# Two attention layers on one core: constants and casts in parts, DMA transposes for the later row tiles, and a new order table

## The chip, the cores and the metric

The kernel runs on one core of one Trainium2 chip. The metric is device time in microseconds of one execution; the time before is the median of three runs. One execution was also recorded by the hardware profiler, and every line of a profile shown here is from such a record.

## The reference

Inputs are q, k and v of shape 4 x 8 x 768 x 64 (batch, heads, rows, head size) in float32, and the weights of a second layer. The first layer is attention with a window: a row sees the 8 first keys (the global ones) and the 96 keys up to its own. A slope per head times the distance is taken off the scores.

```python
keep = is_global | is_local
dist = np.where(is_global & ~is_local, float(n_local), np.abs(rel))
scores = np.where(keep, scale * q @ k.T - slopes * dist, -1e9)
x = softmax(scores) @ v            # then heads side by side: 4 x 768 x 512
```

The second layer is a mixture of four attention experts of head size 64 with causal attention over all rows. A gate picks two experts per row, and their outputs are weighted with the softmax of the two gate values.

```python
q, k, v = x @ wq[e], x @ wk[e], x @ wv[e]
ye = softmax(causal(q @ k.T / 8)) @ v @ wo[e]
out += w[row, e] * ye              # for the two experts of the row
```

## The kernel before

The 4 x 768 rows are 24 row tiles of 128 rows, numbered u = 0 to 23, six per batch. Each tile runs through the same stages, and each stage is a small function with a two-letter name.

First layer: load k, q and v of the tile (lk, lq, lv), 256 KB each; cast them to float16 (kc, qc, vc); transpose k and q on TensorE into PSUM and copy both into kqT (tk, tq; `turn`, L266 and L275); local scores in two halves with the bias added by a matmul (sa, sb; L335, L342, exponential at L345); global scores for up to three tiles at a time (gs); values (vg, va, vb; L356, L371), with the division by the row sum at L378 and L380, which gives x16. Transposed x is made by `turn_x` (tx; L386 on TensorE, copy at L390).

Second layer: keys and queries of the four experts (pk, pq; L401, copy at L406), values and gate logits (pv; L415, L417, L421), the routing in small steps (ro), causal scores in up to three parts (ca, cb, cc; L446, exponential at L449), the mask (ma; L461 on GpSimd), values (za, zb; L474) and the weighting L481, L483 and L485, which gives zs. Transposed zs is made by `turn_z` (tz; L491, copy at L495). The output projection (ou; L502, copy at L505) ends with a store issued from SyncE (L506).

The order of all work is written out in a table of slots, `ORDER`; the tile framework keeps this order on every engine and adds the waits. A slot is a stage, a number and, where the stage has a choice, a letter for the engine: a is ScalarE, g is GpSimd, v is VectorE; for loads s is SyncE's DMA queue and a is ScalarE's. So `tx5v` transposes x of tile 5 and has the copy done by VectorE. What stands earlier in the table stands earlier in the queue of every engine that it uses; a wait holds back what follows on that engine alone.

The weights are loaded by wi and cast by wc. In the kernel before, row kp*4+ko of a weight goes to partition kp, so a partition reads 1 KB in a row, and `turn_x` picks every fourth column of x to match:

```python
issue(w32s[i][:, :, :, :].rearrange("p e k d -> p e (k d)"),
      (moe_wk, moe_wq, moe_wv)[i].rearrange("e (kp ko) d -> kp e (ko d)", ko=NK))
```

Constants are made at the start: the bias of the local scores (xb), and in one function the mask and bias of the global keys, the mask of the keys and the selection matrix (xg), all on VectorE. Buffers `abuf` are zeroed on VectorE (az). `keep_warm` (wm) runs matmuls whose result is not used. PSUM tiles for transposes, projections and outputs share two buffers (psT). After the table a check of all row sums (L753 to L763) decides whether a general path, which is not taken here, has to run.

## Time and profile before

| what | value |
|---|---|
| median of 3 runs | 153.75 us (152.28 to 154.81) |
| the profiled execution | 154.6 us |
| its span | 151.9 us |
| TensorE matmuls | 2987, 137.3 us busy |
| VectorE, ScalarE, GpSimd busy | 111.3, 105.6, 94.6 us |
| DMA | 27.81 MB in 80376 packets |
| transposes on TensorE | 192 of k and q, 96 of x, 48 of z |
| granted TensorE clock | 0.986 |

The span is what the profile covers; the profiled execution is 2.7 us longer than it. TensorE matmuls are pipelined, so the busy time of a run of them is longer than the time that it adds; the spacing of their starts is the better measure. Lines such as L401 are lines of the kernel before. PEld is the loading of a stationary operand, PEq or SPq the sequencer of an engine.

### The profile page before, as it was taken

How to read it: one execution, taken by the hardware profiler on the slowest of the kernel's cores; microseconds unless marked ns; L12 is line 12 of the kernel's file. 1: busy time of each engine (PE TensorE's matmuls, PEld its weight loads, DVE VectorE, ACT ScalarE, POOL GpSimd, SP SyncE). 2: the span in 40 equal slices, each digit the busy share in tenths (PEclk: the TensorE clock that was granted, in tenths of full speed). 3: DMA queues.
4: the chain of work that ended last, by engine and by line, in shares of the span. 5: the costliest groups of instructions: out<-in, count | busy, mean ns of one | idle time of the engine just before them, and what ended most of it. 6: DMA issues, size and time to landing. Idle time of an engine off the chain costs nothing.

```text
span 151.9 us, 7115 instructions
## 1 busy us (share of the span) xinstructions
PE 137.3 (90%) x2987; PEld 107.5 (71%) x2987; DVE 111.3 (73%) x343; ACT 105.6 (70%) x174; POOL 94.6 (62%) x258
## 2 busy tenths in 40 slices
PE   5889969989999998899999999999999999999700
PEld 4556747768789786787787887788868987856300
DVE  6976958577887984888759788797867787797610
ACT  0345656666879887498786877869796988898410
POOL 4492896484888785749889789543786444544000
PEclk9999999999999999999999999999999999999995
DMA  4999999979899898999994994345013003116540
GB/s 106 284 288 291 353 231 279 265 177 277 195 276 233 199 239 184 204 285 223 316 242 103 261 222 135 84 147 134 4 69 145 4 4 140 73 48 230 194 167 11
DMA packets 80376, 27.81 MB, mean 183 GB/s; under 512 B 75472, under 2 KB 77008, under 8 KB 80336
## 3 DMA queue, kind: packets, MB, share of 16 engines
q1 hardware_dynamic: 65632, 23.60, 60.0%
q10 hardware_dynamic: 14704, 3.68, 10.8%
q8 instruction: 25, 0.41, 1.1%
q14 instruction: 15, 0.12, 0.3%
HBM read 20.98 MB, written 6.29 MB: 180 GB/s over the span
## 4 chain that ended last, share of the span: by engine, by line
PE 61%; DMA 11%; DVE 9%; POOL 9%; issue 3%; ACT 2%; POOLq 0%; ACTq 0%; DVEq 0%
DMA qf<-in_q_dram 11%; PE pps L401 10%; PE zps L474 7%; PE ops L502 7%; PE vps L415 6%; PE cps L446 6%; PE zps L371 4%; PE sps L335 4%; POOL vbuf L258 4%; PE tp L266 4%; PE xps L386 3%; PE sps L342 3%; PE ztps L491 2%; PE zps L356 2%; POOL s16q L250 1%
## 5 line engine op out<-in xcount | busy, mean ns | idle before, releaser
L449 ACT ACTIVATE a<-cps 128x1024 f16<-128x1024 f32 (+1 forms) x48 | 42.0, 916 | 4.0 <-PE cps L446 3.6
L258 POOL CAST vbuf<-vf 64x256 f16<-64x256 f32 x92 | 37.0, 402 | 6.6 <-DMA vf<-in_v_dram 2.6
L345 ACT ACTIVATE abuf<-sps 128x636 f16<-128x636 f32 (+1 forms) x48 | 30.7, 683 | 9.1 <-PE sps L342 8.7
L461 POOL TENSOR_SCALAR_AFFINE_SELECT a<-a 128x256 f16<-128x256 f16 x48 | 18.4, 411 | 12.8 <-ACT a L449 12.8
L275 DVE COPY kqT<-tp 128x1024 f16<-128x1024 f16 x23 | 15.5, 686 | 5.3 <-PE tp L266 5.1
L380 DVE TENSOR_TENSOR x<-zps,rinv 128x512 f16<-128x512 f32 x24 | 16.6, 691 | 0.8
L474 PE MATMUL zps<-v2buf,a 128*128 128x65 f16 x336 | 15.4, 193 | 0.2
L371 PE MATMUL zps<-vbuf,abuf 64*128 64x65 f16 x704 | 15.2, 189 | 0.0
L335 PE MATMUL sps<-biasT,ident 64*64 64x318 f16 (+1 forms) x192 | 14.8, 313 | 0.1
L401 PE MATMUL pps<-xT,wk 128*128 128x128 f16 x192 | 14.6, 219 | 0.1
L401 PE MATMUL pps<-xT,wq 128*128 128x128 f16 x192 | 14.5, 219 | 0.0
L474 PEld LDWEIGHTS <-a 128*128 128x128 f16 x336 | 12.9, 97 | 2.1 <-DVE zs L485 0.8
L371 PEld LDWEIGHTS <-abuf 64*128 64x128 f16 x704 | 13.9, 94 | 0.6
L342 PE MATMUL sps<-kqT 64*64 64x159 f16 (+2 forms) x384 | 14.2, 228 | 0.0
L415 PE MATMUL vps<-wvg,xT 128*128 128x260 f16 x96 | 13.6, 275 | 0.0
L502 PE MATMUL ops<-wo,zt 128*128 128x512 f16 x48 | 13.2, 380 | 0.4 <-DVE zt L495 0.4
L250 POOL CAST s16k<-kf 128x512 f16<-128x512 f32 x17 | 10.3, 609 | 5.2 <-DMA kf<-in_k_dram 3.3
L446 PE MATMUL cps<-kq,kq 64*128 64x128 f16 x240 | 13.2, 217 | 0.0
L446 PEld LDWEIGHTS <-kq 64*128 64x128 f16 x336 | 9.9, 94 | 4.5 <-issue 3.4
L401 PEld LDWEIGHTS <-wk 128*128 128x128 f16 x192 | 11.5, 98 | 1.8 <-issue 0.2
L342 PEld LDWEIGHTS <-kqT 64*64 64x64 f16 x384 | 11.4, 108 | 1.1 <-issue 0.2
L401 PEld LDWEIGHTS <-wq 128*128 128x128 f16 x192 | 11.6, 98 | 0.1
(112 smaller groups left out, 272.9 us busy)
## 6 DMA issues: line engine op xcount, KB each, us to landing
out_dram<-osb SPq DMA_DIRECT2D x24, 256.0 KB, 2.1
qf<-in_q_dram SPq DMA_DIRECT2D x20, 256.0 KB, 5.0
vf<-in_v_dram SPq DMA_DIRECT2D x20, 256.0 KB, 5.2
kf<-in_k_dram SPq DMA_DIRECT2D x18, 256.0 KB, 5.1
kf<-in_k_dram ACTq DMA_DIRECT2D x6, 256.0 KB, 5.3
vf<-in_v_dram ACTq DMA_DIRECT2D x4, 256.0 KB, 5.8
qf<-in_q_dram ACTq DMA_DIRECT2D x4, 256.0 KB, 6.0
w<-in_moe_wk_dram SPq DMA_DIRECT2D x1, 512.0 KB, 5.1
```

Source lines behind the costliest of these rows:

```text
L258: copies[on](o[hf * KB:(hf + 1) * KB, c, :, 0:Dh], fs["v", u][c * KB:(c + 1) * KB, hf * HG:(hf + 1) * HG, :])
L335: mm(s_ps[o, hh, 0:2 * w].rearrange("r (c n) -> r c n", c=2), lhsT=ident2[r, :], rhs=biasT[r, p, 0:w].unsqueeze(1).to_broadcast([KB, 2, w] ...
L342: mm(s_ps[o, hh, c * w:c * w + n], lhsT=kqT[b][r, 0, p, k0:k0 + KB], rhs=kqT[b][r, 1, p, k0:k0 + n], start=False, stop=True, skip_group_ch ...
L345: S_.activation(as_[u][:, :, g, :].rearrange("r h (c n) -> r h c n", c=2)[:, :, :, 0:w], s_ps[:, :, 0:2 * w].rearrange("r h (c n) -> r h c ...
L371: mm(zs_[u][:, hf, hq * VW:(hq + 1) * VW], lhsT=as_[u - prev][r, hq % 2, hq // 2, at:at + P], rhs=held("vbuf", u - prev)[r, c, hq, :], sta ...
L401: mm(p_ps[:, i, ep, :], lhsT=w[:, ko, ep, :, :].rearrange("r a d -> r (a d)"), rhs=xT[:, ko, :], start=(i == 0 and ep == 0 and ko == 0), s ...
L415: mm(v_ps[:, :], lhsT=xT[:, ko, :], rhs=wvg16[:, ko, :], start=(ko == 0), stop=(ko == NK - 1))
L446: mm(s_ps[:, e2, i, :], lhsT=kqs[b * NT + ci][r, 0, ep, :], rhs=kqs[u][r, 1, ep, :], start=(i == 0), stop=True, skip_group_check=True)
L449: S_.activation(a2[:, :, 4 * c:4 * c + len(part), :], s_ps[:, :, 0:len(part), :], func=Exp, scale=sc2)
L461: G.affine_select(out=d, in_=d, pattern=[[0, NEP], [1, P]], channel_multiplier=-1, base=0, compare_op=Alu.is_ge, fill=0.0)
L474: mm(z_ps[:, e, :], lhsT=a2[:, e % 2, (e // 2) * n + ci, :], rhs=held("v2buf", b * NT + ci)[:, e, :], start=(e == 0 and ci == 0), stop=Tru ...
L502: mm(o_ps[:, :], lhsT=zts[u][:, ep, :], rhs=wo16[:, ep, :], start=(ep == 0), stop=(ep == NEP - 1))
```

## The change

Constants: the two constant functions are cut into smaller stages (xb, xi, xm, xc, xk, xs), most with a letter for the engine, and the index for the upper 64 rows is made by a second iota instead of an addition. `local_zeros` takes a letter. The value cast is cut into two stages of two halves each (vc and vx).

Transposes: `turn`, `turn_x` and `turn_z` take the letter s, which issues one DMA transpose from SyncE's queue, from SBUF to SBUF, with no PSUM tile and no copy. The table uses it for x and z of tiles 12 to 22, and for q and k of tiles 16 to 23. Since it takes columns as they stand, the weights are now loaded with row ko*128+kp on partition kp, in pieces of 256 bytes, and TensorE's transposes of x take plain columns as well. x16 gets 5 buffers and xT 4 (3 each before). The general path uses the weights of the fast path instead of its own copies.

Table: `ORDER` is written anew. Of the loads, 28 are issued from ScalarE's queue instead of 14. `xt` (the early request for the exponential's table) stands last.

```diff
@@ -72,62 +72,71 @@
     sel = const.tile([P, H // 2, KB], F16)
     warm = const.tile([P, 1], F32)
     V.memset(warm[:, :], 0.0)
+    engines = {"g": G, "v": V}
     rel_i = const.tile([P, W], I32)
-    G.iota(rel_i[:, :], pattern=[[1, W]], channel_multiplier=-1, base=0)
+    for r in (slice(0, KB), slice(KB, P)):
+        G.iota(rel_i[r, :], pattern=[[1, W]], channel_multiplier=-1, base=0)
     row_i = const.tile([P, 1], I32)
     G.iota(row_i[:, :], pattern=[[0, 1]], channel_multiplier=1, base=0)
     col_i = const.tile([P, P], I32)
     G.iota(col_i[:, :], pattern=[[1, P]], channel_multiplier=0, base=0)
 
     def bias_constants(_):
-        up = slice(KB, P)
-        V.tensor_copy(rel[0:KB, :], rel_i[0:KB, :])
-        V.tensor_scalar(rel[up, :], rel_i[up, :], float(KB), None, op0=Alu.add)
+        V.tensor_copy(rel[:, :], rel_i[:, :])
         ge = const.tile([P, W], F32, name="ge")
         V.tensor_scalar(ge[:, :], rel[:, :], 0.0, None, op0=Alu.is_ge)
         lt = const.tile([P, W], F32, name="lt")
         V.scalar_tensor_tensor(lt[:, :], rel[:, :], float(NL), ge[:, :],
                                op0=Alu.is_lt, op1=Alu.mult)
         V.tensor_scalar(lt[:, :], lt[:, :], -1.0, -NEG, op0=Alu.add, op1=Alu.mult)
-        V.tensor_scalar(rel[up, :], rel[up, :], slopes[1] / slopes[0], None, op0=Alu.mult)
+        V.tensor_scalar(rel[KB:P, :], rel[KB:P, :], slopes[1] / slopes[0], None, op0=Alu.mult)
         for p in range(NP):
             V.scalar_tensor_tensor(biasT[:, p, :], rel[:, :], -slopes[2 * p] / sc1, lt[:, :],
                                    op0=Alu.mult, op1=Alu.add)
-        for r in (slice(0, KB), up):
-            V.tensor_copy(ident2[r, :], ident[r, r])
-
-    def global_constants(_):
-
+
+    def half_identities(_, on):
+        for r in (slice(0, KB), slice(KB, P)):
+            copies[on](ident2[r, :], ident[r, r])
+
+
+    def global_mask(_, on):
+        e = engines[on]
         key_i = const.tile([P, 1], I32, name="key_i")
         V.tensor_scalar(key_i[:, :], row_i[:, :], NG - 1, None, op0=Alu.bitwise_and)
         key_f = const.tile([P, 1], F32, name="key_f")
         V.tensor_copy(key_f[:, :], key_i[:, :])
-        col_f = const.tile([P, P], F32, name="col_f")
-        V.tensor_copy(col_f[:, :], col_i[:, :])
         grel = const.tile([P, P], F32, name="grel")
-        V.tensor_scalar(grel[:, :], col_f[:, :], key_f[:, :], None, op0=Alu.subtract)
+        e.tensor_copy(grel[:, :], col_i[:, :])
+        e.tensor_scalar(grel[:, :], grel[:, :], key_f[:, :], None, op0=Alu.subtract)
         g_lo = const.tile([P, P], F32, name="g_lo")
-        V.tensor_scalar(g_lo[:, :], grel[:, :], 0.0, NEG, op0=Alu.is_ge, op1=Alu.mult)
-        V.scalar_tensor_tensor(gmask[:, :], grel[:, :], float(NL), g_lo[:, :],
-                               op0=Alu.is_lt, op1=Alu.mult)
+        e.tensor_scalar(g_lo[:, :], grel[:, :], 0.0, NEG, op0=Alu.is_ge, op1=Alu.mult)
+        e.tensor_scalar(grel[:, :], grel[:, :], float(NL), None, op0=Alu.is_lt)
+        e.tensor_tensor(gmask[:, :], grel[:, :], g_lo[:, :], op=Alu.mult)
+
...
+    def selection(_, on):
+
+        G.memset(sel[:, :, :], 0.0)
         for hq in range(HG):
             at = hq // 2 * 32 + hq % 2 * NG
-            V.tensor_copy(sel[:, hq, at:at + NG], ident2[:, 0:NG])
+            copies[on](sel[:, hq, at:at + NG], ident2[:, 0:NG])
 
 
     rinv1 = const.tile([P, B, NT, H], F32)
@@ -146,13 +155,12 @@
         issue = queues[on]
         if i == 4:
             w32s[i] = wst.tile([P, NK, E], F32, name="wg32", tag="wg32", bufs=1)
-            issue(w32s[i][:, :, :].rearrange("p k e -> p (k e)"),
-                  moe_w_gate.rearrange("(kp ko) e -> kp (ko e)", ko=NK))
+            issue(w32s[i][:, :, :], moe_w_gate.rearrange("(ko kp) e -> kp ko e", kp=P))
             return
         w32s[i] = wst.tile([P, E, NK, Hd], F32, name="w32", tag="w32")
         if i < 3:
-            issue(w32s[i][:, :, :, :].rearrange("p e k d -> p e (k d)"),
-                  (moe_wk, moe_wq, moe_wv)[i].rearrange("e (kp ko) d -> kp e (ko d)", ko=NK))
+            issue(w32s[i][:, :, :, :],
+                  (moe_wk, moe_wq, moe_wv)[i].rearrange("e (ko kp) d -> kp e ko d", kp=P))
         else:
             issue(w32s[i][:, :, :, :].rearrange("p e k d -> p (e k d)")
                   .rearrange("p (a m) -> p a m", a=NEP),
@@ -213,9 +221,9 @@
 
     abufs = [big.tile([P, 2, 2, WA], F16, name=f"abuf{i}") for i in range(NA)]
 
-    def local_zeros(i):
-        V.memset(abufs[i][:, :, :, W:2 * P], 0.0)
-        V.memset(abufs[i][:, :, :, 2 * P + W:WA - KB], 0.0)
+    def local_zeros(i, on):
+        engines[on].memset(abufs[i][:, :, :, W:2 * P], 0.0)
+        engines[on].memset(abufs[i][:, :, :, 2 * P + W:WA - KB], 0.0)
 
     ring("vbuf", NV, [2, HG, VW], Dh)
     ring("v2buf", NV2, [E, VW], Hd)
@@ -249,30 +257,32 @@
         s16s[nm, u] = pp.tile([P, H, Dh], F16, name="s16" + nm)
         copies[on](s16s[nm, u][:, :, :], fs[nm, u][:, :, :])
 
-    def cast_v(u, on):
-
-
-        o = take("vbuf", u)
+    def cast_v(u, x, on):
+
+
+
+        o = held("vbuf", u) if x else take("vbuf", u)
         for hf in range(2):
-            for c in range(2):
+            for c in (hf ^ x,):
                 copies[on](o[hf * KB:(hf + 1) * KB, c, :, 0:Dh],
                            fs["v", u][c * KB:(c + 1) * KB, hf * HG:(hf + 1) * HG, :])
 
     def turn(u, i, on=None):
 
+
+        b, ri = divmod(u, NT)
+        if b not in kqT:
+            kqT[b] = pp.tile([P, 2, NP, S], F16, name="kqT", bufs=2)
+        s16 = s16s["kq"[i], u][:, :, :].rearrange("j h d -> j (h d)")
+        if on == "s":
+            nc.sync.dma_start_transpose(kqT[b][:, i, :, ri * P:(ri + 1) * P], s16)
+            return
         if i == 0:
             tps[u] = psT.tile([P, 2, NP, P], F16, name="tp", tag="t")
         for p in range(NP):
-            nc.tensor.transpose(
-                tps[u][:, i, p, :],
-                s16s["kq"[i], u][:, 2 * p:2 * p + 2, :].rearrange("j h d -> j (h d)"),
-                ident[:, :])
-        if i == 0:
-            return
-        b, ri = divmod(u, NT)
-        if ri == 0:
-            kqT[b] = pp.tile([P, 2, NP, S], F16, name="kqT", bufs=2)
-        copies[on](kqT[b][:, :, :, ri * P:(ri + 1) * P], tps[u][:, :, :, :])
+            nc.tensor.transpose(tps[u][:, i, p, :], s16[:, p * P:(p + 1) * P], ident[:, :])
+        if i == 1:
+            copies[on](kqT[b][:, :, :, ri * P:(ri + 1) * P], tps[u][:, :, :, :])
 
     def global_keys(b):
 
@@ -376,17 +386,20 @@
             z4 = zs_[u][:, :, 0:HG * VW].rearrange("r a (h d) -> r a h d", h=HG)
             rinv = rinv1[:, b, ri, :].rearrange("r (a h) -> r a h", a=2)
             V.reciprocal(rinv, z4[:, :, :, Dh])
-            x16s[u] = pp.tile([P, 2, HG, Dh], F16, name="x16")
+            x16s[u] = pp.tile([P, 2, HG, Dh], F16, name="x16", bufs=5)
             V.tensor_tensor(x16s[u][:, :, :, :], z4[:, :, :, 0:Dh],
                             rinv.unsqueeze(3).to_broadcast([P, 2, HG, Dh]), op=Alu.mult)
 
     def turn_x(u, on):
+
+        xTs[u] = pp.tile([P, NK, P], F16, name="xT", bufs=4)
+        x16 = x16s[u][:, :, :, :].rearrange("r a h d -> r (a h d)")
+        if on == "s":
+            nc.sync.dma_start_transpose(xTs[u][:, :, :], x16)
+            return
         x_ps = psT.tile([P, NK, P], F16, name="xps", tag="t")
         for j in range(NK):
-            nc.tensor.transpose(x_ps[:, j, :],
-                                x16s[u][:, :, :, :].rearrange("r a h d -> r (a h d)")
-                                .rearrange("r (c k) -> r k c", k=NK)[:, j, :], ident[:, :])
-        xTs[u] = pp.tile([P, NK, P], F16, name="xT")
+            nc.tensor.transpose(x_ps[:, j, :], x16[:, j * P:(j + 1) * P], ident[:, :])
         copies[on](xTs[u][:, :, :], x_ps[:, :, :])
 
     def project_qk(u, i, on=None):
@@ -486,12 +499,16 @@
                         ce[:, :].unsqueeze(2).to_broadcast([P, E, Hd]), op=Alu.mult)
 
     def turn_z(u, on):
+        zts[u] = pp.tile([P, NEP, P], F16, name="zt")
+        if on == "s":
+            nc.sync.dma_start_transpose(zts[u][:, :, :],
+                                        zss[u][:, :, :].rearrange("r e d -> r (e d)"))
+            return
         zt_ps = psT.tile([P, NEP, P], F16, name="ztps", tag="t")
         for ep in range(NEP):
             nc.tensor.transpose(zt_ps[:, ep, :],
                                 zss[u][:, 2 * ep:2 * ep + 2, :].rearrange("r e d -> r (e d)"),
                                 ident[:, :])
-        zts[u] = pp.tile([P, NEP, P], F16, name="zt")
         copies[on](zts[u][:, :, :], zt_ps[:, :, :])
 
     def output(u, on):
...
 ORDER = """
-wi4a lq0s qc0g lk0a kc0g wm17 tk0 lv0a lk1a vc0g lq1s xt0 lk2s xb0 xg0 kc1g lq2a lk3a lq3s lq4s
-qc1g tq0a wm12 vs0 az0 gi0 tk1 tq1v lk4a gs0 wm3 gs1 kc2g lv1s az1 az2 lk5s wm1 sa0 lv2s qc2g
-sb0 kc3v lq5a qc3v qc4g tk2 tq2v tk3 tq3v vg0 wi0s wi1s va0 vb0 az3 az4 kc4g kc5v vc1g gs2 lv3a
-lv4s vc2g sa1 sb1 wc0g tk4 wc1g tq4v vg1 sa2 sb2 lk6s wi2s va1 qc5a vb1 sa3 sb3 tx0v tk5 tq5v
...
-sb22 ou10v ou11a vg21 vc21g va21 vc22g vb21 ro5 sa23 sb23 vc23g pv18v pk18 za13 ro5 zb13 pq18a
-ro5 ro5 pv19v ca16 ca17 ro5 ro5 vg22 va22 ro5 ma14 tz12v pk19 pq19v tx21a ca18 vb22 cb16 pk20
-pq20v tx22v vg23 cc16 va23 vb23 pv20a ro6 pv21a cb17 cc17 ma15 ro6 ma16 ro6 za14 tz13v zb14
-pk21 ma17 pq21v ou12a za15 zb15 ou13a ma18 tx23v ca19 ca20 ro6 tz14v ro6 tz15v za16 zb16 pv22v
-pv23a cb20 ca21 ro6 ro6 za17 tz16v ro7 ro7 zb17 ou14a pk22 ma19 pq22v ro7 ro7 cb21 za18 zb18
-pk23 pq23a ro7 ma20 tz17v ro7 ca22 za19 zb19 ro7 cb22 ma21 ou15v ou16v ca23 za20 zb20 tz18v
-cc22 ou17v cb23 za21 zb21 ou18a tz19v ma22 cc23 za22 tz20v tz21a zb22 ou19a ou20v ma23 za23
-tz22v zb23 ou21a ou22a tz23v ou23a
+lk0s az0v xc0v xb0 xi0a lk1s lq0a kc0a az1g az2v az3g xs0g lv0s xm0g vc0v vx0v lq1s lq2a kc1g
+lq3a lk2s wm17 tk0 qc0a qc1v wm7 tq0a lk3a xk0g gi0 kc2g lk4s wm8 vs0 tk1 qc2v lq4s qc3g tq1v
+az4g gs0 wm2 gs1 vg0 kc3v kc4g lv1s lq5a sa0 tk2 tq2v sb0 va0 tk3 tq3v qc4g vc1g lk5a lv2s wi0s
+gs2 vb0 vx1v sa1 wi1a kc5g qc5g vc2g sa2 tk4 tx0v tq4v sb1 sb2 lv3s wc0g lv4a vg1 wi4s wi2s va1
+vb1 sa3 sb3 lk6s vx2v tk5 tq5v tx1v vg2 lq6a va2 vc3g vb2 vx3g gs3 vc4g sa4 wm1 sa5 wc1v tx2v
...
+va10 vc12g vx12g vb10 ca6 tz1v tq16s lk18a lk19s ro1 wc3v ro1 pk8 pq8v sa13 sa14 kc16g vg11
+va11 qc17g vb11 pv7a vs2 pv8v lq19a tk16s za2 tx9v sb13 sb14 qc18g ro1 vc13g ou0v kc17g vx13g
+lk20a zb2 ro1 tq17s pk9 tq18s kc18g pq9a pv9v cb5 vg12 va12 vb12 ca7 ro2 tx10v tx11v cc5 tk17s
+vc14g vg13 va13 vb13 lv15a ro2 ou1v pk10 pq10a ma4 vx14g za3 zb3 sa15 sb15 ro2 ro2 pv10v tx12s
+tz2v za4 zb4 lq20s lq21a tx13s sa16 sb16 qc19g tq19s ro2 kc19g kc20v pk11 ma5 ro2 lq22s tz3v
+pq11a lv16a vg14 va14 vb14 tk18s tk19s ca8 cb8 pv11v pv12v za5 gs7 zb5 lv17s lv18a tx14s tz4v
+ma6 ro2 ro3 ma7 vc15g vx15g tk20s qc20g sa17 sb17 ro3 ou2v vg15 va15 vb15 ca9 cb9 ou3v pk12
+vc16g za6 zb6 ro3 ro3 pq12v lv19s ou4v lk21a vx16g tx15s ma8 ca10 vg16 tq20s qc21g qc22g ro3
+vc17g vx17g cb10 va16 vb16 pk13 pq13a tz5v ro3 sa18 tx16s sb18 za7 zb7 tz6v vc18g vx18g gi3
+pk14 pq14v ca11 cb11 tz7v za8 zb8 pv13v pv14v cc10 ro3 lq23s tq21s kc21g ma9 lk22s lk23a vc19g
+tk21s vx19g vg17 va17 vb17 tx17s vs3 gs8 ou5v ro4 lv20a ou6v za9 zb9 ca12 ca13 pk15 pq15v ma10
+tz8v kc22g kc23g cc11 ma11 tk22s vg18 va18 vb18 sa19 pv15a lv21s qc23g pv16v sa20 tq22s sb19
+ro4 tq23s vc20a za10 zb10 tk23s pv17v tz9v sb20 ca14 vg19 va19 vb19 ou7v ou8v ca15 vx20g vg20
+va20 ro4 ro4 ro4 tx18s tx19s vb20 ma12 cb14 pk16 pq16a sa21 sb21 vc21v tz10a ma13 za11 ro4 ro4
+ro5 zb11 vx21v gs9 pk17 pq17v lv22s ro5 tz11a ro5 lv23s ca16 vg21 va21 tx20s cb15 vb21 ro5 ou9v
+ro5 tx21s pk18 pq18v vc22g sa22 vx22g sb22 vc23g za12 zb12 tz12s pk19 pq19v cb16 cc16 za13
+ou10a zb13 tz13s pk20 pq20v ca17 vg22 va22 vb22 ou11a ou12v vx23g ma14 ro5 sa23 sb23 za14 zb14
+pv18a tx22s pv19v ma15 ma16 ro5 cb17 cc17 ou13v za15 zb15 pv20v ro6 pv21a ca18 ca19 ro6 vg23
+ma17 va23 vb23 pk21 pq21a pv22v za16 zb16 ro6 ca20 cb20 ro6 ma18 ro6 tx23v ro6 ro6 tz14s pk22
+pq22a ma19 ma20 tz15s tz16s za17 zb17 ou14a tz17s pv23v ro7 ca21 ro7 cb21 za18 zb18 ou15v tz18s
+ro7 ro7 pk23 pq23a za19 zb19 ca22 ou16v ca23 ro7 ro7 za20 ma21 zb20 tz19s ou17v cb22 cc22 ro7
+za21 zb21 tz20s ou18v tz21s ma22 cb23 cc23 ma23 ou19v za22 zb22 tz22s ou20a za23 zb23 ou21a
+tz23v ou22a ou23v xt0
 """
```

## The prediction

> **What bounds the kernel now.** I read the page first, parts 1 and 2, to see which engine has no room and whether that holds all the way.
>
> ```profile
> PE 137.3 (90%) x2987; PEld 107.5 (71%) x2987; DVE 111.3 (73%) x343; ACT 105.6 (70%) x174; POOL 94.6 (62%) x258
> PE   5889969989999998899999999999999999999700
> PEclk9999999999999999999999999999999999999995
> DMA  4999999979899898999994994345013003116540
> ```
>
> One slice is 3.8 us. TensorE is full from about slice 17 on; before that it has dips, and the DMA engines are at nine tenths. So there are two stages: up to about 62 us loads and start-up decide, after it TensorE. The windows of the trace put numbers on the second stage:
>
> ```profile
> 62.00:108.00 46.00, 45.48 (x1083) 36.94 (x1082) 36.31 (x101) 36.02 (x61) 33.70 (x89) 1.00 0.74 188
> 108.00:145.00 37.00, 35.57 (x720) 26.48 (x714) 28.20 (x103) 30.14 (x47) 17.69 (x58) 1.00 0.27 100
> ```
>
> The columns are window, its length, busy time of PE, PEld, DVE, ACT and POOL, granted clock, DMA share and GB/s. TensorE is busy 81.05 of 83 us. Busy time of pipelined matmuls overstates, so I price them by the chain of work that ended last, whose pieces give the spacing of a run:
>
> ```profile
> 39.72 0.57 PE tp L266 x8
> 57.92 4.76 DMA qf<-in_q_dram
> 79.63 0.45 PE tp L266 x8
> 99.69 0.89 PE pps L401 x16
> 100.58 0.61 PE zps L474 x20
> 110.80 0.54 PE ops L502 x2
> 142.95 0.29 PE ztps L491 x2
> 143.26 0.29 DVE zt L495
> ```
>
> Eight transposes in 0.45 us are 56 ns each, as are the projections (0.89/16). Priced in this way for every form, all matmuls need about 119 us of the 143 us between the first and the last. From 65 to 140 us each 5 us window holds 4.2 to 4.7 us of such work: the rest is waits under half a microsecond. The chain has a long DMA piece at 57.9 us and none after it, so I set the boundary of the stages at 62 us. The last two lines show the end: each link there is a transpose, a copy, a projection.
>
> **What the Trainium skill says.** "VectorE: DVE Perf Modes", The three transpose paths, gives 390 ns for a 128x128 transpose on TensorE and 1309 ns through the DMA crossbar. The trace's TensorE transposes last 219 ns alone and cost 56 ns in a run, so the 390 is no price for removed work here. "DMA: Bandwidth & Descriptors", Latency and other measured facts, gives 261 GB/s for a DMA transpose, 350 to 400 GB/s where contiguous. The same page, Issuing engines are not separate DMA queues, says that SP's and ACT's transfers share 16 engines; the trace agrees, as loads from either queue land after 5.0 to 6.0 us in the median. No transposing DMA is in the trace of before.
>
> **The change, part by part.**
>
> (1) Transposes leave TensorE. x of 11 tiles is 44 instructions, z of 11 is 22, q and k of 8 are 64: 130 x 56 ns = 7.3 us, all in the second stage. Their copies go too: 8 kqT at 0.69, 9 xT at 0.42 and 10 zt at 0.29 are 12.2 us on DVE, and 2 xT and 1 zt are 1.5 us on ACT. Neither engine bounds, so I count nothing for the copies. **-7.3 us.**
>
> (2) The 38 DMA transposes that replace them. Here the trace shows nothing, so I bound them. Low: 128 KB at 261 GB/s are 0.50 us of all engines. Nearest row: the trace's 256-byte packets take 18 ns, and 512 of them over 16 engines are 0.58 us. High: if the writes go as 32-byte pieces, 4096 of them at the 9 ns that the trace's smallest packets take, over 16, are 2.3 us. I take 0.6 us; z is half. That is 27 x 0.6 + 11 x 0.3 = 19.5 us of engine time. The second stage has 46 x 0.26 + 37 x 0.73 = 39 us free, so it fits. Time to landing: at least the 2.1 us of an output, at most the 5 us of a load when loads are queued ahead.
>
> Cover: I summed the TensorE work in the new table between each transpose and its first reader. It is 4.2 to 17 us for q and k, 3.7 to 10 us for x, 4 to 5 us for z of 12 and 13, and 1.6 to 4.0 us for z from 14 on. A landing of 3 us is hidden for q, k and x. Tiles 16 and 17 of k and q and tile 12 of x come while loads still fill the engines and have 4 us: I add **+1.0 us** for them (0 to 4).
>
> (3) SP's queue. The transposes are all on it, in order. Behind each stand loads and output stores. In the stretch that answers to 62 to 108 us it holds 41 entries: 24 transposes, 8 loads, 9 outputs. Two outputs that follow each other take 0.95 us to issue, so 17 of them take 8 us, and 24 transposes may take up to (46 - 8)/24 = 1.6 us each before the queue itself bounds. A transpose that waits for its source holds back loads; these are for tiles two and more ahead, so nobody waits yet. I take 0 us. SP's queue before spends its time waiting, not issuing:
>
> ```profile
> SPq L506 <- ACT osb L505: 28.8, 11, 10.3
> SPq L506 <- DVE ce L483: 11.1, 3, 10.3
> ```
>
> (4) The end. From z of tile 17 on, stores and transposes alternate on SP: z of 20 stands behind the store of tile 17, which waits for its projection and a 0.69 us copy. From the last values of tile 22 to its projection there are 1.7 us of TensorE work; needed are reciprocal, weight and scaling on DVE (0.18 + 0.16 + 0.42) and a DMA of 2.1 us, so TensorE waits about 1.2 us; at tile 20 somewhat less. The link of before (transpose 0.29, copy 0.29) is gone for it, but tile 23 keeps it. **+1.5 us** (0 to 4).
>
> (5) Start. Before, DVE builds all constants in a row from 1.3 to 10.2 us, the selection last; the first local scores start at 13.0. After, copies, masks and memsets lie on ACT, POOL and DVE together, the 0.84 us int32 shift is gone, and the first k comes ahead of the gate weights. TensorE's work ahead of the first scores is some 8.5 us from 1.6 us. But the first four loads must still come, and then loads decide (the chain holds three long pieces of q loads, at 14.4, 24.8 and 57.9 us). I take **-1.0 us** (-3 to +1). The table load of ACT, 1.28 us, is no longer asked for early; at its first use it falls where ACT waits for loads, so 0 (0 to 1.3).
>
> (6) Weights in 256-byte packets instead of 1 KB: 2048 x 18 ns against 512 x 50 ns, over 16 engines: 2.3 against 1.6 us, three times +0.7, all in the load-bound stage. About half is on the path: **+1.0 us** (0 to 2).
>
> (7) Other moves. Value casts: 74 of 96 halves stay on POOL, 18 go to DVE, 4 to ACT. DVE gets about 5 us of casts, 7 more output copies (4.8), 5 more v copies (2.1) and 12 weight casts (about 4), and loses 7 q and k casts (3.4) and the 12.2 of (1), with some 4 us of constants: it ends near 107 us. ACT loses some 9 us of copies and gains 15 DMA issues of about 0.4 us. Neither reaches TensorE's load; 0 us. Three more keep-warm matmuls of 0.2 us lie in the start's waits. The general path is not run: 0.
>
> Sum: -7.3 + 1.0 + 1.5 - 1.0 + 1.0 = **-4.8 us**. The profiled execution took 154.6 us, 151.9 of it the span; that gives 149.8. The median of the runs is 0.85 below the profiled one: **149.0 us**, 3.1% faster.
>
> **The rivals.**
>
> *Given back.* The work leaves TensorE but the time returns in waits: x and k land after 5 us while loads fill the queue, and the end has waits of 2 us at three tiles. For it: the DMA share of 0.74 from 62 to 108 us and 4.9 us landings there. Against: the distances of (2). Then (2) costs 3 and (4) 3 us: -7.3 + 3 + 3 - 1 + 1 = -1.3, 152.4 us, no measurable change.
>
> *The crossbar or its queue becomes the bound: slower.* One x, q or k transpose costs more than about 1 us of the engines or of SP. The price at which it decides: the second stage has 39 us free, minus 6 us at its very end that nobody can use, over 27 + 11/2 = 32.5 units, is 1.0 us. At 1.3 us, one crossbar figure of the skill, the second stage needs 44 + 32.5 x 1.3 = 86 us of DMA where TensorE needs 76; with imperfect overlap (3 us) the end goes to 62 + 86 + 3, 13 us after TensorE's 138: about 160 us. At the high bound of 2.3 us it would be beyond 190. For it: 32-byte pieces, and an order that is strict on SP. Against: the 261 GB/s.
>
> *The table does not do better.* Loads still decide up to 62 us and further because transposes delay loads; then TensorE starves early in the second stage. It would give about the time of before, and I count it with the first rival.
>
> **How the numbers follow.** Forecast case 57% (145 to 150.7), given back 18% (150.7 to 156.8), slower 25%, of which 20% about 160 and 5% far above. A measurement of this kernel can tell about 2% from no change, so the chances are 0.57, 0.18 and 0.25. The range leaves out a few per cent below 145 and the upper part of the last case: 145 to 160. The likeliest case alone has 145 to 150.7.
>
> **What would show it.** Right: 130 fewer matmuls at the three transposing lines, the priced TensorE work near 112 us, transposing DMAs landing in about 2 to 3 us, the chain in TensorE through the second stage, waits of TensorE on a z transpose only in the last 10 us. Wrong: chain pieces of SP or of a transposing DMA between 62 and 130 us, landings over 4 us at a time without loads, transposes that follow each other by over 1.5 us on SP, or gaps over 1 us ahead of the local scores of 15 to 22. The first local scores at 11 to 12 us would show (5) right.

## The result and the profile after

The changed kernel takes 162.73 us (median of 4 runs, 160.84 to 164.01) against 153.94 us for the kernel before on the same chip: a ratio of 1.057, 95% interval 1.041 to 1.073. It is slower. The forecast was 149.0 us, with 145 to 160. Each ratio leaves out the runs over 1.5% above the fastest of their kernel, so it can differ a little from that of two medians, which are of all runs.

The profiled execution took 162.38 us, its span is 160.2. First the page of the changed kernel: busy time of TensorE, then the 40 slices (one is 4.0 us here).

```profile
PE 133.2 (83%) x2860; PEld 101.9 (64%) x2860; DVE 108.6 (68%) x328; ACT 99.3 (62%) x160; POOL 94.0 (59%) x258
PE   5949959889999999999559998959999799984500
PEclk9987999999999999999987999977999999999975
...
PE 51%; DMA 22%; DVE 9%; POOL 9%; issue 3%; ACT 1%; ACTq 0%; POOLq 0%
```

TensorE has less to do, as forecast, but its row has holes where before it had none: slices 19 and 20 (76 to 84 us), 26 (104 to 108 us), and the last ones. The clock dips in slices 20 and 21 and in 26 and 27 (the first slice is 0). DMA is 22% of the chain that ended last. The two windows that were shown of before:

```profile
62.00:108.00 46.00, 39.49 (x891) 30.33 (x883) 31.03 (x96) 29.17 (x47) 31.45 (x83) 0.95 1.24 212
108.00:153.00 45.00, 38.65 (x802) 28.36 (x794) 30.98 (x103) 31.18 (x48) 17.78 (x58) 0.98 0.59 152
```

From 62 to 108 us TensorE is busy 39.5 of 46 us where it was busy 45.5, at a clock of 0.95, and the DMA share is 1.24 instead of 0.74 (packets that overlap on an engine count twice, so it can pass 1). In the chain of work that ended last, these are pieces of after 62 us:

```profile
75.14 6.07 DMA xT<-x
102.00 4.58 DMA xT<-x
117.81 4.14 DMA xT<-x
141.38 4.26 DMA zt<-zs
147.84 2.30 DMA zt<-zs
```

Each is a DMA transpose, and the pieces of 75 and 102 us are those ahead of the two holes. The waits of TensorE name the readers (engine, operation, line, what it waited for: us in total, times, longest):

```profile
PE vps L428 <- DMA xT<-x: 5.0, 2, 3.0
PE tp L283 <- POOL s16k L258: 3.6, 2, 2.1
PE ops L519 <- DMA zt<-zs: 3.3, 3, 2.2
PE nps L763 <- DVE ones L761: 2.1, 1, 2.1
```

The two at L428 are the value projections of tiles 12 and 17 (pv12v, pv17v).

**The accounts.** I priced every matmul with the spacing that its form has in the kernel before. This gives the kernel before 112.2 us where the chain pieces of the prediction gave about 119; another average of the spacings moves the effects below by up to 1 us, so only the differences are used. From that price and the starts in the trace:

| | before | after | effect |
|---|---|---|---|
| all priced work | 112.2 us | 104.2 us | -8.0 |
| of it done by 65 us | 41.6 | 40.6 | +1.0 |
| done from 65 to 135 us | 63.5 | 52.4 | +11.1 |
| left at 135 us, and the time it takes | 7.1 in 9.7 us | 11.2 in 18.3 us | +4.5 |
| last matmul starts at | 144.7 us | 153.3 us | +8.6 |

The effects sum to 8.6 us. From 65 to 135 us, waits of TensorE over 0.3 us (from start to start, less the price; the idle times of the profile's lines are 0.1 to 0.2 us shorter each) are 0 before and 8.8 us after; two stretches of 3.4 us at half clock behind the longest waits, which cost up to 1.7 us each, cover the rest of the 11.1. So the gain that was forecast came in full, and three places gave back twice as much.

**Where the transposes are late.** SyncE's queue in the changed kernel (start, us, operation):

```profile
62.95 2.89 SPq L278 DMA_TRANSPOSE kqT<-s16q  x1
65.88 0.59 SPq L238 DMA_DIRECT2D kf<-in_k_dram  x1
66.57 2.64 SPq L278 DMA_TRANSPOSE kqT<-s16k  x1
...
75.14 1.27 SPq L398 DMA_TRANSPOSE xT<-x  x1
76.45 0.58 SPq L238 DMA_DIRECT2D qf<-in_q_dram  x1
77.53 2.81 SPq L398 DMA_TRANSPOSE xT<-x  x1
```

A load occupies the queue for 0.6 us, a transpose for at least 1.2 us, and up to 2.9 us here. Added up over 62 to 108 us, SyncE issues for 42.0 of 46 us (20 transposes 33.4 us, 15 others 8.6 us); before it was 22.3 us. x of tile 12 is made by this instruction of the chain:

```profile
69.09 0.69 DVE x L390
```

So it was ready at 69.8 us, was issued 5.4 us later, landed 6.1 us after that (the first line of the chain above), and its reader needed it then at once. For x of 12 to 20 the way from ready to landed is 6.6 to 14.1 us.

ScalarE has a hole at the same time (its timeline; a gap and what ended it in brackets):

```profile
76.60 0.59 ACT L419 CAST kq<-pps 128x512 f16<-128x512 f32 x1
81.28 0.37 ACTq L238 DMA_DIRECT2D vf<-in_v_dram  x1
81.70 1.51 ACT L462 ACTIVATE a<-cps 128x1024 f16<-128x1024 f32 x2 [4.51 <-DMA xT<-x]
```

It does nothing from 77.2 us until it issues a load at 81.28 us, and that is 0.08 us after x of tile 12 has landed. The load has nothing to do with x. But the records of the DMA issues show that all of them use eight completion semaphores in turn, and this load and that transpose have the same one. From 62 us on, 8 of the 9 loads that ScalarE issues start within 0.08 us of the landing of the DMA that had their semaphore before. The Trainium skill says in "DMA: Bandwidth & Descriptors", Anatomy of one DMA, that a DMA engine doesn't wait on semaphores: the wait is in the issuing sequencer. The trace agrees. ScalarE's causal exponentials stood behind this one for 4.1 us; behind the others it stood 1.1 us at most.

### The profile page after: what moved, and what is told of

It is laid out like the page before. It is cut to its first block, busy times and chain, and to the rows that moved or that the text cites. A ratio compares the mean times of both kernels' runs of the same rounds, so it can differ in the third digit from the quotient of the medians.

```text
span 160.2 us, 6913 instructions
## 1 busy us (share of the span) xinstructions
PE 133.2 (83%) x2860; PEld 101.9 (64%) x2860; DVE 108.6 (68%) x328; ACT 99.3 (62%) x160; POOL 94.0 (59%) x258
## 4 chain that ended last, share of the span: by engine, by line
PE 51%; DMA 22%; DVE 9%; POOL 9%; issue 3%; ACT 1%; ACTq 0%; POOLq 0%
PE pps L414 10%; DMA xT<-x 9%; DMA zt<-zs 6%; PE cps L459 5%; PE vps L428 5%; PE tp L283 5%; PE ops L519 5%; PE zps L381 4%; PE zps L487 4%; PE sps L345 4%; DMA kf<-in_k_dram 4%; POOL vbuf L267 3%; PE sps L352 3%; DMA kqT<-s16q 3%; PE zps L366 2%
## 5 line engine op out<-in xcount | busy, mean ns | idle before, releaser
L462 ACT ACTIVATE a<-cps 128x1024 f16<-128x1024 f32 (+1 forms) x48 | 42.0, 915 | 14.1 <-PE cps L459 8.1
L267 POOL CAST vbuf<-vf 64x256 f16<-64x256 f32 x74 | 30.0, 406 | 4.3 <-DMA vf<-in_v_dram 1.3
L258 POOL CAST s16k<-kf 128x512 f16<-128x512 f32 x20 | 12.4, 626 | 11.6 <-DMA kf<-in_k_dram 11.5
L428 PE MATMUL vps<-wvg,xT 128*128 128x260 f16 x96 | 14.3, 280 | 5.0 <-DMA xT<-x 5.0
L522 DVE COPY osb<-ops 128x512 f32<-128x512 f32 x18 | 12.2, 686 | 7.7 <-PE ops L519 6.4
L519 PE MATMUL ops<-wo,zt 128*128 128x512 f16 x48 | 14.3, 391 | 3.3 <-DMA zt<-zs 3.3
L381 PE MATMUL zps<-vbuf,abuf 64*128 64x65 f16 x704 | 15.7, 191 | 0.1
L285 DVE COPY kqT<-tp 128x1024 f16<-128x1024 f16 x15 | 10.3, 688 | 7.2 <-PE tp L283 7.2
L258 POOL CAST s16q<-qf 128x512 f16<-128x512 f32 x21 | 12.8, 618 | 3.2 <-DMA qf<-in_q_dram 3.0
L459 PE MATMUL cps<-kq,kq 64*128 64x128 f16 x240 | 13.9, 220 | 0.0
L428 PEld LDWEIGHTS <-xT 128*128 128x128 f16 x96 | 8.5, 98 | 8.1 <-DMA xT<-x 5.4
```

Source lines behind the costliest of these rows:

```text
L258: copies[on](s16s[nm, u][:, :, :], fs[nm, u][:, :, :])
L267: copies[on](o[hf * KB:(hf + 1) * KB, c, :, 0:Dh], fs["v", u][c * KB:(c + 1) * KB, hf * HG:(hf + 1) * HG, :])
L381: mm(zs_[u][:, hf, hq * VW:(hq + 1) * VW], lhsT=as_[u - prev][r, hq % 2, hq // 2, at:at + P], rhs=held("vbuf", u - prev)[r, c, hq, :], sta ...
L428: mm(v_ps[:, :], lhsT=xT[:, ko, :], rhs=wvg16[:, ko, :], start=(ko == 0), stop=(ko == NK - 1))
L459: mm(s_ps[:, e2, i, :], lhsT=kqs[b * NT + ci][r, 0, ep, :], rhs=kqs[u][r, 1, ep, :], start=(i == 0), stop=True, skip_group_check=True)
L462: S_.activation(a2[:, :, 4 * c:4 * c + len(part), :], s_ps[:, :, 0:len(part), :], func=Exp, scale=sc2)
```

## The experiments

### Which transposes cost

Four kernels put transposes of the new table back on TensorE, with the copy on VectorE, one kind each and all of them; a fifth runs the table of before in the changed kernel.

```diff
 a1: x, z, q and k        a2: z only      a3: q and k only      a4: x only
-tx12s ... tx22s    +tx12v ... tx22v    (x; some 1 us of TensorE work after vb of the tile)
-tz12s ... tz22s    +tz12v ... tz22v    (z; as much after zb of the tile)
-tk16s tq16s ...    +tk16 tq16v ...     (q, k; at the later of the two slots)
 d1: ORDER of before, with xg cut into the new stages, vx behind each vc
```

> All 38 DMA transposes go back to TensorE with a copy by VectorE; table, constants, casts, loads and weights stay those of the kernel after. Theory (the transposing DMAs cost the time: they fill SP's queue and slow the loads from 62 us on): 151 to 155 us, about the kernel before, since the priced TensorE work is again near 120 us. Rival A (the new table, the constants, the loads from ScalarE or the 256-byte weights cost it): 159 us or more. Rival B (only the z transposes at the end cost it): 155 to 158 us, of which the z alone explain most.

> Only the z transposes of tiles 12 to 22 go back to TensorE; q, k and x stay with the DMA. Theory: 157 to 160 us: the wait of 2.4 us and the waits of the last 10 us go, the losses from 62 to 110 us stay. Rival A: 162 us. Rival B: 154 us.

> Only the q and k transposes of tiles 16 to 23 go back to TensorE (16 of the 38 DMA transposes, all of those issued before 75 us). Theory: 154 to 158 us: x of tile 12 no longer stands behind five transposes on SP and the loads are slowed less; the wait of 3.1 us at 78 us and the half clock after it go. Rival A: 164 us, since TensorE gets 3.6 us of work back. Rival B: 163 us.

> Only the x transposes of tiles 12 to 22 go back to TensorE. Theory: 156 to 159 us: the two waits on x (3.1 and 2.2 us) and the two stretches of half clock of 3.4 us after them go, 2.5 us of TensorE work come back; SP's queue and the loads are still crowded by q and k. Rival A: 164 us. Rival B: 162 us.

> The table of the kernel before, every transpose on TensorE, with the rest of the change kept: weights in 256-byte pieces, constants in parts (selection and masks on VectorE as before, the mask of the keys on GpSimd), x16 with 5 and xT with 4 buffers. Theory (these parts are neutral; the table without the DMA transposes it was planned for, and the DMA transposes, are what costs): 152.5 to 155.5 us. Rival A (the weights' 256-byte pieces and the constants cost several us): 157 us or more.

Measured: all back 167.3 us (1.089, 1.082 to 1.096); z back 161.8 (1.044, 1.034 to 1.054); q and k back 161.5 (1.039, 1.029 to 1.049); x back 157.6 (1.026, 1.020 to 1.033); table of before 155.6 (1.011, 1.004 to 1.017).

Only x alone is a clear step, 5.2 us; z alone and q and k alone stay above the ranges that the theory gave them. In the trace of a4 (x alone) no wait of TensorE over 2 us and no half clock is left between 17 and 146 us. The old table in the new kernel costs 1.6 us over the kernel before: that is the part of the weights' layout, the constants and the buffers. All transposes back on TensorE is the slowest of all, against my expectation: from 62 us on TensorE waits 0.3 to 0.8 us ahead of the transposes of 14 tiles, 7.6 us in all, mostly for copies on VectorE. That the new table has no room for these copies (VectorE, and the two buffers psT) is my reading of it. So the table can't be judged apart from the transposes that it was planned for, and the steps of a2, a3 and a4 don't add up to that of a1.

### The transfers, or those who wait for them

Both kernels have q and k on TensorE as in a3, and at the 16 old slots a DMA of the same tile into a buffer that nobody reads: c1 a plain copy, c2 a transpose.

```diff
+    def plain(u, i, on=None):
+        scr = pp.tile([P, H * Dh], F16, name="scr", bufs=3)
+        dma(scr[:, :], s16s["kq"[i], u][:, :, :].rearrange("j h d -> j (h d)"))
 c2:     nc.sync.dma_start_transpose(scr[:, :, :], ...)
```

> q and k of tiles 16 to 23 are transposed by TensorE as in a3, and at the 16 slots of their DMA transposes SP issues a plain DMA of the same 128x512 tile into a scratch tile that nobody reads. Theory D (the issue of a transpose, 1.2 us of SP each, and what it does to SP's order): a plain DMA issues in some 0.5 us, so within 1 us of a3, 160.5 to 162.5 us. Rival E (bytes on the DMA engines): as much slower than a3 as the next kernel.

> As c1, but SP issues a DMA transpose into the scratch tile that nobody reads. Whatever it is above a3 and c1 is what 16 transposes cost everybody else, with no reader waiting. Theory D: 2 to 5 us above c1, by x issued later on SP. Rival E: 2 us or more above a3 in both c1 and c2. If c2 is within 1 us of c1, neither SP nor the engines lose from a transpose as such, and what costs is only the reader that waits for it.

Measured: 159.1 us (1.032, 1.023 to 1.042) and 159.5 us (1.030, 1.021 to 1.039). c1's lines (issue min/median/max, then issue to landing):

```profile
L289 SPq DMA_DIRECT2D scr<-s16q x8: 470/565/1772, 63.3 to 102.4; - x8
...
DMA to landing us min/median/max: 2.0/3.7/4.8
```

and those of c2:

```profile
L289 SPq DMA_TRANSPOSE scr<-s16q x8: 1205/1244/2209, 61.1 to 105.6; - x8
...
DMA to landing us min/median/max: 3.4/4.7/7.6
```

"Advanced Engine Details and Errata", X-Bar Transpose, in the Trainium skill has it that transposing DMAs are as fast as regular ones. For single tiles of 128 KB they are not here: a transpose costs SyncE 1.24 us in the median where a copy of the same 128 KB costs 0.57, and lands after 4.7 us instead of 3.7. Still both kernels take the same time, and no more than a3 without these DMAs, though SyncE issues for 39.1 of the 46 us from 62 to 108 us in c2 and for 30.1 in c1. So a full queue and more traffic alone cost nothing that can be seen here. What costs, by this, is that someone waits. The comparison has a limit: against the changed kernel TensorE does 64 transposes more (3.6 us at 56 ns each), which also moves every reader later. In c2 x of tile 12 still takes 8.5 us from ready to landed (11.4 in the changed kernel), and yet the longest wait of TensorE from 62 to 140 us is 1.0 us.

### SyncE's issues and ScalarE's loads

b1 casts q and k of a tile into one buffer and transposes both in one DMA of 256 KB, 8 issues fewer; this buffer is there 5 times, where q and k had 3 each. b2 issues 10 of SyncE's loads among the transposes from ScalarE instead, so that the transposes are issued earlier.

```diff
 b1
-            nc.sync.dma_start_transpose(kqT[b][:, i, :, ri * P:(ri + 1) * P], s16)
+            nc.sync.dma_start_transpose(
+                kqT[b][:, :, :, ri * P:(ri + 1) * P].rearrange("r i p j -> r (i p) j"),
+                s16j[u][:, :, :, :].rearrange("j i h d -> j (i h d)"))
 b2: from tq16s on, every load lk/lq/lv with the letter s gets the letter a
```

> The kernel after with q and k of tiles 16 to 23 cast into one tile and transposed by one DMA of 128x1024 in place of two of 128x512: 8 DMA transposes fewer on SP, the same bytes. Theory D (SP's issue time of 1.2 us per transpose and the order on its queue decide when x lands): SP is 10 us less busy, x of tile 12 is issued some 5 us earlier, 157 to 160 us. Rival E (what the transposes do to the 16 DMA engines decides: bytes, slowed load packets): the same bytes, so 161.5 to 164 us, and the issue of the merged one takes about twice as long.

> The kernel after with the 10 loads that stand on SP's queue among the DMA transposes issued from ScalarE instead; same slots, same bytes. Theory D (SP's queue): SP is 6 us less busy between 62 and 120 us and a transpose no longer waits behind a load that waits for its buffer; 158 to 161 us. Rival E (the DMA engines): unchanged within 1%, 161.5 to 164 us.

Measured: b1 160.3 us (1.035, 1.027 to 1.043), b2 164.1 us (1.051, 1.043 to 1.058). A merged transpose can be issued in 1.24 us, as one of 128 KB (from 1.19) or the 64 KB of z (from 1.17), so the least price is one of the instruction. But the eight merged ones take SyncE 17.9 us where the sixteen took 26.0, and from 62 to 108 us its queue is still full (39.2 of 46 us). In b1 only 1 of 9 loads of ScalarE starts at a landing, and the hole at 76 to 84 us is gone; waits of 1.1 and 0.7 us between 98 and 102 us stay, with half clock behind them. So b1 has three things that the changed kernel has not: fewer issues, more buffers for the casts, and other pairs of DMAs on one semaphore. It can't tell them apart.

b2 doesn't gain, as it should have if SyncE's order were all: SyncE issues for 33.1 of the 46 us there. In its trace ScalarE stands at loads 4.0 us until x of tile 12 has landed and 3.1 us until a transpose of k has, and TensorE waits 2.4, 1.4 and 1.3 us for ScalarE. No run takes ScalarE's loads back to SyncE or gives them semaphores of their own, so what the shared semaphores cost by themselves is not shown.

### Half clock

```diff
-pv12v                  -pv17v                  -ou19v
+wm14 pv12v             +wm10 pv17v             +wm10 ou19v
```

> The kernel after with 14, 10 and 10 more keep-warm matmuls ahead of the values of tile 12, the values of tile 17 and the output of tile 19, the three places where TensorE waited over 2 us for a DMA transpose; nothing else changes. Theory (a wait on a transpose costs twice: its own length, and the half clock of 3.4 us that follows): the half-clock stretches at 82 and 106 us go, 1.5 to 4 us faster than the kernel after, 158.5 to 161 us. Rival C (the waits alone cost, the clock does not matter): 162.5 to 165 us, since the extra matmuls delay work or do nothing.

Measured: 159.3 us (1.031, 1.025 to 1.037), 3.4 us less than the changed kernel. In its trace the stretches at 82 and 106 us are gone; one stands at 101 us, behind a wait of 2.1 us for transposed q and k. "TensorE: Matmul & The Clock Gate", Part 1, in the Trainium skill gives half rate after at least one idle window of some 3.4 us. The stretches at half clock inside the traces last 3.41 us or twice that, but most of the waits ahead of them are shorter, so here the measurement goes: from 62 to 146 us of all twenty traces TensorE waits 18 times for 2.0 to 3.7 us, and after 16 of these waits half clock sets in, before 3.5 us have passed from their end. The two without it are a wait of 2.2 us for z in the changed kernel (143.5 us) and one of 3.1 us in g3 below. Half of 3.4 us is 1.7 us: so much more than itself can a wait cost (3.4 us where the stretch is twice as long), and matmuls without use in the wait take such a part back.

### Mending hold by hold

f1 moves the first readers of x of 12 and 17 later, by about 3.7 and 3.1 us of TensorE work. g1 adds buffers for the casts to that. f2 mends the end alone: the last output copy on ScalarE, xt at the start. f3 is f1 and f2 with z of 17 to 22 on TensorE.

```diff
 f1: pv12v moved behind ou3v, pv17v moved behind cb14
 f2: -ou23v -xt0 (last)      +ou23a +xt0 (ahead of kc0a)
 g1: f1, and
-        s16s[nm, u] = pp.tile([P, H, Dh], F16, name="s16" + nm)
+        s16s[nm, u] = pp.tile([P, H, Dh], F16, name="s16" + nm, bufs=6)
```

> The changed kernel with two slots of the table moved: the first readers of transposed x of tiles 12 and 17 (pv12v, pv17v) stand about 3.7 and 3.1 us of TensorE work later. Every DMA and every transpose stays as it is. Theory of the near readers (a transpose is ready for use 8 to 14 us after its source, TensorE stands 5.3 us at these two readers and then runs 3.4 us at half clock after each): 157.5 to 160 us, and no wait of over 1 us at either reader. Rival, the transposes slow everything through the shared DMA engines or SP's queue: 161.5 to 163.5 us, the wait comes back at the next reader.

> The changed kernel with the copy of the last output on ScalarE in place of VectorE and the request for the exponential's table at the start; all transposes stay. The theory that late z and the last copy share the loss at the end: 160.5 to 162 us (1 to 2 us less than the changed kernel). The rival, that the last copy alone is the end's loss: 159 to 160 us; that it is nothing: 162.5 to 163.

> The two moved readers of the first kernel of this call, the end of the second, and z of tiles 17 to 22 transposed on TensorE; x of 12 to 22, q and k of 16 to 23 and z of 12 to 16 stay with the DMA engines. If x by DMA is worth its 44 TensorE instructions (2.5 us) once its readers stand later: 150.5 to 153 us, below the kernel before by 1 to 2%. If what is gained is given back at other readers of x: 153.5 to 156 us.

> f1_later_readers with 6 buffers in place of 3 for the cast keys and queries. In that kernel TensorE's wait did not go away: at 74.5 us VectorE stands 2.4 us on a cast of keys whose buffer an unissued DMA transpose still holds, and the copies behind it hold TensorE back 1.9 us at 75.9 us. If the loss is a chain of such single holds: 157.5 to 160 us with these buffers, and no wait of over 1 us before 85 us. If SP's queue as a whole is late there, the next reader (global scores of keys and queries of 18) waits instead: 160.5 to 162.5 us.

Measured: f1 161.7 us (1.054, 1.042 to 1.066), f2 161.0 (1.048, 1.037 to 1.060), f3 156.8 (1.019, 1.008 to 1.029), g1 163.0 (1.054, 1.042 to 1.066).

f1 is what my theory was wrong about. x of 12 now has 7.4 us to spare and x of 17 3.0 us, and next to nothing is won. TensorE's waits in f1:

```profile
PE vps L428 <- DVE zt L512: 1.7, 1, 1.7
...
PE gps L323 <- ACT a L462: 1.4, 1, 1.4
```

Both lie at 76 to 81 us, where the hole was, and the half clock comes again. Behind the first stands this wait of VectorE in f1:

```profile
DVE s16k L258 <- DMA kqT<-s16k: 2.4, 1, 2.4
```

A cast of keys needs a buffer that a transpose not yet done still reads; the copies behind it on VectorE come late, and with them TensorE's value projection. Behind the second stands ScalarE in f1, held at a load's issue until x of 12 has landed:

```profile
ACT a L462 <- DMA xT<-x: 3.8, 1, 3.8
```

So the reader was one of three holders of the same lateness. g1 takes the buffer's wait away as well, and no time is won: TensorE now waits longer for ScalarE at the same place (2.5 us in f3, which has f1's readers):

```profile
PE gps L323 <- ACT a L462: 2.8, 1, 2.8
```

Taking holders away one by one moves the wait along. In all kernels that keep x and the separate transposes of q and k on the DMA engines (the changed one, a2, b2, b5, f1, f2, f3, g1), ScalarE stands 3.3 to 5.3 us until x of tile 12 has landed.

f2 is worth 1 to 2 us, no clear step in itself. f3 is 4.9 us below f1, so late z on TensorE and the last copy together are worth about what the accounts show for the end. f3 and g1 came out above both of their ranges: what the readers, the buffers and the end were thought to give did not come in full.

### Fewer transposes, and a kernel that keeps some

a6 has x of 12 to 22 and z of 17 to 22 on TensorE and the end of f2; q, k and z of 12 to 16 stay with the DMA engines. g2 is a6 with b1's merged transpose. g3 is f3 with it: it differs from g2 in x, which goes by DMA with later readers. h1 starts from the kernel before: q and k of 19 to 23 merged by DMA, z of 12 to 17 by DMA.

```diff
 a6: -tx12s ... tx22s -tz17s ... tz22s  +tx12v ... tx22v +tz17v ... tz22v  +ou23a  xt0 first
 h1: ORDER of before, -tk19 tq19v ... +td19 ...   -tz12v ... tz17v  +tz12s ... tz17s
```

> From the kernel after: x of tiles 12 to 22 and z of tiles 17 to 22 on TensorE, the copy of the last output by ScalarE in place of VectorE, the early table load at the start in place of the end; q and k of 16 to 23 and z of 12 to 16 stay with the DMA. Theory (waits for x cost some 5 us, waits for the late z and the last copy on VectorE some 3 us, q and k with their long distance nothing): 153 to 156 us. Rival (q and k cost too, by slowing the loads): 157 us or more, as a4.

> a6_late_fixed with keys and queries of a tile cast into one buffer and transposed by one DMA of 256 KB (8 issues on SP fewer, some 10 us of SP's time). If SP's time still costs something there: 152 to 153.5 us, at or below the kernel before. If it does not: 153.5 to 155 us as before.

> f3_readers_and_end with keys and queries of a tile transposed by one DMA, as in b1_merged_qk; against g2_few_and_merged it differs in x of 12 to 22 (by DMA here, on TensorE there) and in the two later readers of x. In the traces a load issued from ScalarE in the stretch of the transposes starts within 0.1 us of the landing of an earlier DMA, 9 times of 11 in the changed kernel and once of 10 in b1_merged_qk: ScalarE stands at the issue, 4.1 us at 81.3 us. If late transposes on SP and ScalarE held at such issues are what x by DMA costs: 152.5 to 154.5 us, below both, as 2.5 us of TensorE's work are gone. If x by DMA is worth nothing here even so: 155.5 to 157.5 us.

> The kernel before (its table, weights and constants) with q and k of tiles 19 to 23 cast into one tile and transposed by one DMA each, issued 1.2 us of TensorE work after the casts (8.8 to 13 us ahead of the first reader), and z of tiles 12 to 17 by DMA (5.5 us or more ahead of the output projection). Takes 2.9 us of work off TensorE with 11 DMA transposes. Theory (a DMA transpose costs nothing where its reader is more than 8 us of TensorE work away, or 5 us where no loads come): 150.5 to 153 us. Rival (each transpose slows loads and SP whoever reads it): 154 us or more.

Measured: a6 154.2 us (1.005, 1.001 to 1.009), g2 155.7 (1.009, 1.004 to 1.014), g3 155.2 (1.001, 0.996 to 1.006), h1 156.0 (four runs, 153.5 to 158.3, too wide for a verdict). From 62 us on the counts that g3's expectation names are 8 of 9 and 1 of 9.

a6 shows that x and the end were the loss: without them the kernel is where it was before. g2 gains nothing over a6 and lies above both of its ranges. g3 shows more: of the loss of 5.7% it wins back all but 0.1% with all of x of 12 to 22 still on the DMA engines. By the medians of all runs, which for g3 spread from 152.2 to 159.8 us, it wins back all but 0.8%. Against f3 it has the merged transposes, and with them the 5 buffers and the other pairs on a semaphore. SyncE is not less busy by it (40.8 of the 46 us, 37.3 in f3), but ScalarE no longer stands at the landing of x of tile 12 (3.3 us in f3); which of the three brings 1.9% down to 0.1% is open. The ratio of g3 times the median of before is 154.1 us, in the range that was expected if x by DMA pays; but its median, 155.2 us, lies in neither range, and against g2 the intervals overlap, so a gain from x by DMA is not shown. g3 has 7.1 us of priced work less than the kernel before, and the same time: in its trace a reader waits again, once for 3.1 us at 93 us for merged q and k. Even the fastest run of h1, 153.5 us, is above the 150.5 to 153 us of its theory. None of the kernels beats the kernel before.

## Why the prediction was wrong

**(1) right.** 127 matmuls fewer with three more keep-warm ones are the 130; 7.3 us were forecast, 8.0 us came by the price of before.

**(2) wrong: this is the step that failed.** Its term was +1.0 us (0 to 4); from 65 to 135 us 11.1 us were lost. It took a landing of 3 us from the slot on as hidden by 3.7 us or more of cover. Measured for x are 6.6 to 14.1 us from ready to landed at tiles 12 to 20: 3.7 to 11.1 us until SyncE issues, 2.5 to 6.1 us until it lands. The bounds for the landing (2.1 to 5 us) were near, and so was the packet row of the price: the trace has 512 packets of 256 bytes for each x, q and k, none of 32. The queue ahead of the landing was missing from the sum. And the sum had only readers in it. A late transpose holds also the cast that wants its source buffer, and ScalarE's next load through the semaphore; f1 and g1 show these two. Half clock behind the longest waits, which the changed kernel and f1 show, was not in it at all. What f1 does not show is how the 11.1 us split among the holders.

**(3) wrong, and it feeds (2).** I took 0 us and gave 1.6 us per transpose as the price from which the queue binds. The 20 transposes of 62 to 108 us take 1.67 us each, 1.2 at least, and the queue is full (42.0 of 46 us). "Nobody waits yet" was wrong for buffers and semaphores. c2, with a queue nearly as full of transposes that nobody reads, speaks for a full queue that costs only through those who wait.

**(4) right in kind, a third of the size.** +1.5 us (0 to 4); it was 4.5. TensorE waits 3.3 us for z in three places: 2.2 us for tile 19, 0.8 for tile 12 and 0.2 for tile 22. The step had named tile 22 with 1.2 us and tile 20 with less; z of 19 landed 4.3 us after its issue, not 2.1. Not seen: the last output copy stands on VectorE ahead of the row-sum check, 2.1 us (the last line of the waits above), which f2 and f3 mend. Before it was 0.5 us:

```profile
PE nps L759 <- DVE ones L757: 0.5, 1, 0.5
```

**(5) wrong.** -1.0 us was forecast, to be seen in first local scores at 11 to 12 us; they start at 13.3 to 13.5, and at 13.0 before. The parts of the masks that GpSimd builds stand ahead of its first casts, and wait themselves 2.4 us for VectorE; TensorE's transposes of k wait 2.1 us for them (the longest in the second line of the waits). The other 1.5 us of that line come at 20.4 us, behind a late load of k.

**(6)** is not contradicted: +1.0 us was taken for the weights' layout; d1, which has it together with the constants and the buffers in the old table, is at +1.6 us (0.6 to 2.6), and no run has it alone. **(7)** I took 0 us. Loads moved to ScalarE were counted at their 0.4 us of issue; the 4.1 us that one of them stands there are part of the hole.

**The rivals.** The one that ends slower named 160 us and the queue or the crossbar as bound, deciding from 1.0 us per transpose. Its time was nearest, and SyncE's price was above that point. But it priced throughput of the engines and a queue that ends later. c2 and b2 speak against that as the whole cause: it is latency, with what is queued behind it. That 160 us came so near is in part luck. I gave it 25%, since I held 0.6 us for the price although nothing in the profile before bounded an issue on SyncE.

## What to carry to other kernels

Price a DMA that replaces work of an engine by its way from source ready to landed, with the queue of its issuer in it, and not by its bandwidth: here 7 to 14 us stood where a copy from PSUM took half a microsecond. Then list everything that it holds while it is late, not only its reader: the source buffer and the next cast into it, the destination, and the completion semaphore, which a later and unrelated load may need. A load on a compute engine's queue turns the last of these into idle time of that engine, and a busy TensorE can pay some 1.7 us more for a wait of 2 us or more, since half clock followed 16 of 18 here.

## What the runs showed that I had not expected

- A transposing DMA costs its issuer some 1.2 us at the least, at each size used here: from 1.17 us for 64 KB, 1.19 for 128 KB and 1.23 for 256 KB. A plain DMA of 128 KB costs 0.54 to 0.57 us in the median.
- It lands after 2.3 us when no loads are under way (most z near the end), and among loads after 4.2 to 4.7 us in the median and 7.6 at most (128 KB).
- Beside the transposes the packets of ordinary loads get hardly slower: on ScalarE's queue, which has only loads, 256 bytes take 20.2 ns in the mean from 62 to 108 us, and 18.1 ns in the kernel before.
- Half clock for 3.4 us, or twice that, followed 16 of 18 waits of 2.0 to 3.7 us; it was missing after one of 3.1 us.
- Unrelated DMAs are tied together by eight completion semaphores used in turn.
